# Output projection of the recurrent layer with stationary weights, and its projections emitted in quarters

## The chip, the cores and the metric

The kernel runs on one core of a Trainium2 chip. The metric is the device time of one launch in microseconds; the time before is the median of three runs. A profile is one more execution, taken with the hardware profiler.

## What is computed

Four layers follow one another on x of 2048 rows by 512: A, B, A, B, each on a layer norm of x and added to x.

```python
# layer A: 64 segments of 32 rows, strictly one after the other; M = 8 memory rows, 32 heads of 128
for s in range(n_seg):
    h = concat([mem, x[32*s : 32*s+32]])           # 40 rows
    q, k, v = h @ Wq, h @ Wk, h @ Wv               # 512 -> 32 heads x 128
    p = softmax(mask(q @ k.T * scale))             # 40 x 40 per head
    o = (p @ v) @ Wo                               # 4096 -> 512
    mem = o[:8]; outs.append(o[8:])
# layer B: full attention over 2048 rows, 32 heads of 16
x = x + A(layernorm(x)); x = x + B(layernorm(x))   # and both once more
```

So the memory rows of a segment's result are an input of the next segment's three projections: layer A is a chain of 128 segments in the whole kernel.

## The kernel before

One program holds all four layers. The recurrent chain of layer A is walked segment by segment (`segment`, called by `layer_a`), and the work of layer B is cut into *units* (`emit_qk` L467 and `pv_mm` L487: four score matmuls on four row strips of TensorE, an exponential of 128x2048 in two ScalarE instructions at L481 and L484, and four matmuls that sum up values) which fill the time in which a segment waits. There are 1040 units in all, about half for each B layer. Those of the first run beside the first A layer and, what is left, in a stretch between the A layers; those of the second run beside the second A layer and in a tail after it. Everything that is needed once per 128 rows (layer norm, the rows' projections of layer B, the residual) stands in *chains* (`chain`, `run_chain`), lists of functions that are run one at a time.

TensorE's order is fixed when the program is built. `segment` (L788) holds a list of the segment's steps, `a_pick` takes one of the first six by when its inputs are due on a planner's clock (`Clock`, with one counter per engine), and `step` (L416) decides at every turn whether that step (A), a chain's function (M), a unit's score matmuls (U) or a unit's value matmuls (V) go next. The quota of units per segment comes from the units not yet done. The other engines run in the order in which these functions call them, as far as the scheduler leaves it so. The steps of one segment are, with the index 0 or 1 for the two halves of the 32 heads:

- Q, K, V (`cols` L601): the segment's 32 columns of h are the stationary operand, 512 columns of the weight move, and four such products run in the four 32-column strips of TensorE. Sixteen matmuls make one half of one projection. Its result, 128 rows of 512, is copied out of PSUM by ScalarE or VectorE (`stage`, `evac`).
- X (`turn` L617, `qk_turn` L630): Q and K of a half are turned by eight 128x128 transposes into one PSUM bank and copied by VectorE into `a_KT` and `a_QT`.
- S (`s_group` L646): scores, exponential, row sums, division and 32x32 transposes (L658, L662 to L674).
- P, or A and B where many units are due (`pv_group`, `pv_pair`, `pv_mms` L676): p @ v, four row strips at once, and the copies into `a_OT`.
- O (`o_cols` L707): the product with Wo. The segment's first 32 columns of `a_OT` per head are stationary, 512 columns of Wo move, sixteen matmuls per half, four column strips. Each strip holds the sum over its own eight heads.
- F (`o_fold` L716): the four strips' sums have been copied as fp32 (`a_Op`); four fp32 matmuls with a 0/1 matrix (`c_sel`) add them and turn them, 128 features by 32 rows. VectorE then casts eight of the 32 columns into the next segment's h (L846), and that starts the next segment.

A segment has 40 rows, and a 32-column strip holds 32. The eight rows that don't fit are gathered over four segments: layer norm and projections of these rows in `qk_rest` and the `rest` functions, and for Wo a POOL copy per segment into `a_OX` (L850) and, once per four segments, `o_rest` (two more O rounds, a copy and a fold) at the head of the chain that `tile_done` builds.

```python
PLAN = "Q0 K0 V0 X0 Q1 K1 S0 V1 X1 S1 P0 O0 P1 O1 F0".split()
def o_cols(self, b, rr, lhsT, ready):
    for j in range(4):
        for t in range(4):
            h = 16 * rr + 4 * t + j
            self.nc.tensor.matmul(b.t[32 * t:32 * t + 32, :], lhsT=lhsT(h), rhs=self.Wo[:, h, :], ...)
```

Of the kernel before, what the change touches and what calls it, by code (L numbers as in the profile page):

```python
# [97 lines left out]
class Kern:  # L98
# [21 lines left out]
    def consts(self, mem0):  # L120
# [27 lines left out]
        self.sel32 = cp.tile([128, MAIN], f32, name="c_sel32")  # L148
        nc.vector.tensor_reduce(self.sel32[:], self.identf[:].rearrange("p (t r) -> p r t", t=4), axis=AX.X, op=ALU.add)
# [43 lines left out]
    def a_buffers(self, bp):  # L193
# [16 lines left out]
        self.OX = bp.tile([128, H, 32], bf16, name="a_OX")  # L210
        self.Op = bp.tile([128, 512], f32, name="a_Op")
# [7 lines left out]
    def buffers(self):  # L219
# [4 lines left out]
        self.wbp = self.pool("b_W", bufs=2)  # L224
# [66 lines left out]
    def evac16(self, dst, src, n, ready):  # L291

        self.nc.vector.tensor_copy(dst, src)
        return self.ck.ew("DVE", n // 2, ready)
# [121 lines left out]
    def step(self, ra=INF, ma=None, lead=INF, unit=True):  # L416
# [12 lines left out]
        elif rm <= now and (mode == c.mode() or ma == c.mode() or ra > now or rm < now - 2.5):  # L429
# [139 lines left out]
    def qk_rest(self):  # L569
# [11 lines left out]
        def turn(rr):  # L581
            b, done = self.turn(st[1], st[0])
# [19 lines left out]
    def cols(self, W, lhsT, rr, ready):  # L602

        b, at = self.take()
        for ft in range(4):
# [4 lines left out]
        return b, self.ck.pe(0.87, max(at, ready), "PV", 16) + 0.2  # L610
# [6 lines left out]
    def turn(self, k, q):  # L617
# [3 lines left out]
        for i, (x, _) in enumerate((k, q)):  # L621
            for j in range(4):
                self.nc.tensor.transpose(ps[:, 4 * i + j, :], x[:, 128 * j:128 * j + 128], self.ident[:])  # L623
        return b, self.ck.pe(0.5, max(at, k[1], q[1]), "full", 8)

    def qk_cols(self, h_s, proj, rr):
        b, done = self.cols((self.Wq, self.Wk)[proj], lambda ft: h_s[:, ft, :], rr, self.at.get("mem", 0.0))
        self.staged["QK"[proj], rr] = self.stage(b, done)

    def qk_turn(self, rr):  # L630
        b, done = self.turn(self.staged["K", rr], self.staged["Q", rr])
        ps = b.h(8, 128)
        self.evac16(self.KT[:, rr, :, :, 0:MAIN], ps[:, 0:4].rearrange("p j (t q) -> p j t q", q=MAIN), 512, done)
        b.free = self.at["X", rr] = self.evac16(self.QT[:, rr].rearrange("p j t q -> p j (t q)"), ps[:, 4:8], 512, done)

    def v_round(self, h_s, rr):
        b, done = self.cols(self.Wv, lambda ft: h_s[:, ft, :], rr, self.at.get("mem", 0.0))
        b.free = self.at["V", rr] = self.evac(self.V[:, rr, :], b.t[:], 512, done)
# [68 lines left out]
    def o_cols(self, b, rr, lhsT, ready):  # L707

        for j in range(4):
            for t in range(4):  # L710
                h = 16 * rr + 4 * t + j
                self.nc.tensor.matmul(b.t[32 * t:32 * t + 32, :], lhsT=lhsT(h), rhs=self.Wo[:, h, :],  # L712
                                      start=(rr == 0 and j == 0), stop=(rr == 1 and j == 3), tile_position=(0, 32 * t))
        return self.ck.pe(0.87, ready, "PV", 16) + 0.2

    def o_fold(self, part, ready):  # L716

        b, at = self.take()
        ps = b.f(4, MAIN)
        for ft in range(4):  # L720
            self.nc.tensor.matmul(ps[:, ft, :], lhsT=part[:, 128 * ft:128 * ft + 128], rhs=self.sel32[:], start=True, stop=True)  # L721
        return b, ps, self.ck.pe(0.45, max(at, ready), "full", 4)
# [3 lines left out]
    COST = {"Q": 0.87, "K": 0.87, "V": 0.87, "X": 0.5, "S": 0.5, "P": 0.4, "A": 0.3, "B": 0.3, "O": 0.87, "F": 0.45}  # L726

    def a_ready(self, k, g, left):

        at = self.at  # L730
        if k in "QKV":
            if k != "V" and g and "X0" in left:
                return INF
            t = at.get("mem", 0.0)
        elif k == "X":
            if f"Q{g}" in left or f"K{g}" in left:
                return INF
            t = max(self.staged[p, g][1] for p in "QK")
        elif k == "S":
            if f"X{g}" in left or at["R"] == INF:  # L740
                return INF
            t = max(at["X", g], at["R"])
# [4 lines left out]
        elif k == "O":  # L747
            if f"P{g}" in left or f"A{g}" in left or f"B{g}" in left or (g and "O0" in left):
                return INF
            t = max(at["O", 2 * g], at["O", 2 * g + 1])  # L750
            if g:
                return t
        elif k == "F":
            if "O1" in left:
                return INF
            t = at["part"]
        return max(t, self.bank_at())

    MODE = {"Q": "PV", "K": "PV", "X": "full", "S": "PV", "V": "PV", "P": "S", "A": "S", "B": "S", "O": "PV", "F": "full"}

    def a_pick(self, left):
        now = self.ck.t["PE"] + 0.05
        best = (INF, None)
        for x in left[0:6]:
# [712 lines left out]
```

## Time and profile before

| | before |
|---|---|
| median of three runs | 3594.34 us (3589.13 to 3604.32) |
| the profiled execution | 3603.48 us, span 3601.8 us |
| PE busy | 3118.1 us, 87% of the span |
| ACT busy | 2446.0 us, 68% |
| DVE busy | 1719.0 us, 48% |
| POOL busy | 523.3 us, 15% |
| granted TensorE clock, mean | 0.919 |
| DMA | 371.58 MB, 103 GB/s |

A PE that counts as busy is not at its peak: a matmul's record holds its way through the array, too. The segment's steps can be found by their lines: L608 are Q, K and V, L623 the transposes X, L652 and L658 the scores, L681 the value sums, L712 Wo, L721 the fold. L479, L481, L484 and L493 are the units of layer B, and L465 are matmuls that only keep TensorE at work. A segment reaches from one L846 on DVE to the next.

### The profile page before, as it was taken

What the parts mean: (1) busy time and instruction counts of PE and PEld (TensorE: products, weight loads), DVE (VectorE), ACT (ScalarE), POOL (GpSimd) and SP (SyncE); (2) the same over time, 40 slices, a digit from 0 to 9 for tenths busy, and PEclk for the clock granted to TensorE, in tenths of its full rate; (3) what the DMA queues carried; (4) which work ended last, traced back from release to release, by engine and by line L of the source; (5) the groups of instructions that cost most, each with busy time, mean ns of one, the idle gap of its engine ahead of it and who ended that gap; (6) DMA issues with size and microseconds to landing.
All of it is one profiled execution on the core that took longest, in us unless ns stands there. A gap on an engine that the chain in (4) does not pass through costs nothing.

```text
span 3601.8 us, 136341 instructions
## 1 busy us (share of the span) xinstructions
PE 3118.1 (87%) x59593; PEld 1706.8 (47%) x59611; DVE 1719.0 (48%) x4724; ACT 2446.0 (68%) x3242; POOL 523.3 (15%) x1017
## 2 busy tenths in 40 slices
PE   4888888889898898888898998888988889889898
PEld 2444444444444444444445444444444444446566
DVE  1333333436465655546655553444646565652411
ACT  1333354657676877876698765564867688888898
POOL 1111111112111111111111111111212111110000
PEclk7888888989999998989999998888998999999999
DMA  6111111324243424443524322322425253554331
GB/s 211 37 37 38 49 54 50 101 66 125 88 135 109 148 81 121 139 136 112 154 80 132 96 80 70 91 84 83 137 86 161 85 153 95 167 148 142 106 96 46
DMA packets 375376, 371.58 MB, mean 103 GB/s; under 512 B 72048, under 2 KB 302704, under 8 KB 374768
## 3 DMA queue, kind: packets, MB, share of 16 engines
q1 hardware_dynamic: 334560, 251.31, 24.7%
q0 software_dynamic: 34432, 102.54, 8.4%
q8 instruction: 468, 7.67, 0.9%
q10 hardware_dynamic: 5776, 8.91, 0.8%
q14 instruction: 140, 1.15, 0.1%
HBM read 260.10 MB, written 102.50 MB: 101 GB/s over the span
## 4 chain that ended last, share of the span: by engine, by line
PE 55%; ACT 22%; issue 9%; DVE 8%; DMA 5%; POOL 1%; SPq 0%; ACTq 0%; DVEq 0%; POOLq 0%
PE bank L608 21%; ACT b_pt L481 15%; PE bank L712 9%; PE b_SX L479 7%; PE bank L721 4%; PE b_oacc L493 3%; ACT b_pt L484 3%; DMA b_W<-in_B_wqkv_dram 2%; PE bank L623 2%; PE bank L681 2%; PE bank L1041 1%; ACT a_OT L286 1%; DVE a_PT L672 1%; PE bank L479 1%; DVE a_pn L670 1%
## 5 line engine op out<-in xcount | busy, mean ns | idle before, releaser
L481 ACT ACTIVATE b_pt<-b_SX 128x1536 bf16<-128x1536 f32 (+1 forms) x1040 | 1493.2, 1436 | 429.7 <-PE bank L479 389.1
L484 ACT ACTIVATE b_pt<-bank 128x512 bf16<-128x512 f32 (+1 forms) x1040 | 616.8, 593 | 1.8 <-PE bank L479 1.8
L479 PE MATMUL b_SX<-b_q,b_k 32*128 32x512 bf16 (+3 forms) x4944 | 428.6, 311 | 128.7 <-ACT b_pt L481 110.6
L608 PEld LDWEIGHTS <-a_hT 128*32 128x32 bf16 x12288 | 316.1, 100 | 370.5 <-issue 87.6
L493 PE MATMUL b_oacc<-b_pt,b_v 128*17 128x512 bf16 (+3 forms) x6592 | 422.0, 311 | 12.2 <-ACT b_pt L481 5.8
L479 PE MATMUL bank<-b_q,b_k 32*128 32x512 bf16 (+3 forms) x1648 | 416.1, 312 | 10.2 <-DVE b_xo L1145 5.2
L712 PE MATMUL bank<-a_Wo,a_OT 128*32 128x512 bf16 x4096 | 380.0, 453 | 37.3 <-ACT a_OT L286 34.6
L479 PEld LDWEIGHTS <-b_k 32*128 32x128 bf16 x6592 | 167.7, 92 | 394.4 <-issue 330.4
L608 PE MATMUL bank<-a_Wq,a_hT 128*32 128x512 bf16 x4096 | 299.4, 416 | 15.0 <-DVE a_hT L846 4.8
L288 DVE CAST a_qk<-bank 128x512 bf16<-128x512 f32 x305 | 210.9, 691 | 175.8 <-PE bank L608 158.8
L608 PE MATMUL bank<-a_Wk,a_hT 128*32 128x512 bf16 x4096 | 279.2, 394 | 3.9 <-ACT a_oTa L286 3.9
L608 PE MATMUL bank<-a_Wv,a_hT 128*32 128x512 bf16 x4096 | 265.9, 389 | 12.9 <-ACT a_qk L286 12.6
L288 DVE CAST a_OT<-bank 128x160 bf16<-128x160 f32 x575 | 162.7, 316 | 156.9 <-PE bank L681 155.7
L665 DVE TENSOR_REDUCE a_sm<-a_pn 128x5 f32<-128x200 bf16 x256 | 92.4, 361 | 267.1 <-ACT a_pn L662 266.7
L681 PEld LDWEIGHTS <-a_V 32*128 32x128 bf16 x4096 | 124.8, 93 | 199.8 <-issue 163.2
L943 DVE TENSOR_TENSOR b_ain<-b_oacc,b_ain 128x512 f32<-128x512 f32 (+2 forms) x248 | 164.1, 662 | 103.9 <-PE b_oacc L493 94.0
L712 PEld LDWEIGHTS <-a_OT 128*32 128x32 bf16 x4096 | 126.0, 105 | 183.3 <-issue 54.7
L286 ACT CAST a_qk<-bank 128x512 bf16<-128x512 f32 x207 | 121.1, 587 | 133.6 <-PE bank L608 133.2
L493 PEld LDWEIGHTS <-b_v 128*17 128x17 bf16 x6592 | 126.3, 89 | 169.4 <-issue 127.1
L721 PE MATMUL bank<-c_sel,a_Op 128*128 128x32 f32 x1024 | 163.8, 309 | 44.7 <-ACT a_Op L286 30.7
L721 PEld LDWEIGHTS bank<-c_sel,a_Op 128*128 128x128 f32 x1024 | 149.9, 225 | 97.1 <-ACT a_Op L286 58.5
L948 POOL DMA_DIRECT2D b_A<-b_ain x176 | 95.7, 544 | 675.4 <-DVE b_ain L943 462.2
(139 smaller groups left out, 4484.4 us busy)
## 6 DMA issues: line engine op xcount, KB each, us to landing
b_ain<-b_A SPq DMA_DIRECT2D x224, 256.0 KB
b_W<-in_B_wqkv_dram SPq DMA_DIRECT2D x192, 256.0 KB
b_A<-b_ain POOLq DMA_DIRECT2D x176, 256.0 KB, 2.8
b_q<-b_Q SPq DMA_DIRECT2D x240, 128.0 KB
b_k<-b_K SPq DMA_DIRECT2D x201, 128.0 KB
b_v<-b_V SPq DMA_DIRECT2D x312, 68.0 KB
b_A<-b_aout POOLq DMA_DIRECT2D x80, 128.0 KB, 2.6
a_rest<-a_vx POOLq DMA_DIRECT2D x64, 128.0 KB, 2.2
```

Of the source, the lines that this page charges most:

```text
L286: self.nc.scalar.copy(dst, src)
L288: self.nc.vector.tensor_copy(dst, src)
L479: nc.tensor.matmul(out[t][:, j * qw:(j + 1) * qw], lhsT=k[32 * t:32 * t + 32, kj * 128:(kj + 1) * 128], rhs=q[32 * t:32 * t + 32, 0:qw], s ...
L481: nc.scalar.activation(pt[:, 0:NX, 0:w], self.SX[:, 0:NX, 0:w], ACT.Exp, scale=B_SCALE)
L484: nc.scalar.activation(pt[:, NX + i, 0:w], b.t[:, 0:w], ACT.Exp, scale=B_SCALE)
L493: self.nc.tensor.matmul(self.oacc[32 * t:32 * t + 17, 0:qw], lhsT=u.v[:, kj, 17 * t:17 * t + 17], rhs=u.p[:, t, j * qw:(j + 1) * qw], star ...
L608: self.nc.tensor.matmul(b.t[32 * t:32 * t + 32, :], lhsT=lhsT(ft), rhs=W[:, ft, n * 512:(n + 1) * 512], start=(ft == 0), stop=(ft == 3), t ...
L681: self.nc.tensor.matmul(ps[:, L * h4:L * h4 + L], lhsT=V[32 * t:32 * t + rows, st, h4 * DH:(h4 + 1) * DH], rhs=self.PT[32 * t:32 * t + row ...
L712: self.nc.tensor.matmul(b.t[32 * t:32 * t + 32, :], lhsT=lhsT(h), rhs=self.Wo[:, h, :], start=(rr == 0 and j == 0), stop=(rr == 1 and j == ...
L721: self.nc.tensor.matmul(ps[:, ft, :], lhsT=part[:, 128 * ft:128 * ft + 128], rhs=self.sel32[:], start=True, stop=True)
L943: nc.vector.tensor_tensor(acc[:, w], k.oacc[:, w], acc[:, w], ALU.add)
L948: nc.gpsimd.dma_start(B.Acc_d[self.qc][self.hg][:, self.qo:self.qo + self.qw], acc[:, w])
```

## The change

1. Wo becomes the stationary operand again (`wo_steps`): for every head four 128x128 blocks of Wo are loaded and all 40 columns of `a_OT` move, 128 matmuls per segment that add up in one PSUM bank of 4 x 40 columns. There is no `a_OX`, no `a_Op`, no fold and no `o_rest`; the result stands in PSUM as features by rows, and L846's cast (now L857) reads it directly. The 128 matmuls are four steps W0 to W3 of 32, each for eight heads, ready when those heads' copies into `a_OT` are.
2. Q, K, V and W are emitted in four parts (`col_steps`, `wo_steps`). While a step is open (`active`), a unit's score or value matmuls may go between its parts; a chain's function may only when it has been due for over 2.5 us on the planner's clock.
3. K and Q are turned apart, Y for K and X for Q, each with a PSUM bank of its own; and the copies out of that bank may go to ScalarE where the planner sees it end sooner (`evac16`).
4. The plan is a new one: K before Q, V0 ahead of the first turns, Q1 and V1 behind S0, W0 and W1 behind S1. `a_pick` weighs a step's due time, its place in the list and a change of TensorE's tiling.
5. Buffers: three instead of two for `b_W` (one more load ahead), four instead of two for `a_qk`.

```diff
-        self.OX = bp.tile([128, H, 32], bf16, name="a_OX")
-        self.Op = bp.tile([128, 512], f32, name="a_Op")
...
-        self.wbp = self.pool("b_W", bufs=2)
+        self.wbp = self.pool("b_W", bufs=3)
...
-        self.stp = self.pool("a_stage", bufs=2)
+        self.stp = self.pool("a_stage", bufs=4)
...
     def evac16(self, dst, src, n, ready):
+        ck = self.ck
+        act = max(ck.t["ACT"] - 0.09, ready + 0.04) + ck.cost("ACT", n)
+        dve = max(ck.t["DVE"] - 0.09, ready + 0.04) + ck.cost("DVE", n // 2)
+        if act + self.act_bias < dve - 0.1:
+            self.nc.scalar.copy(dst, src)
+            return ck.ew("ACT", n, ready)
         self.nc.vector.tensor_copy(dst, src)
...
-    def step(self, ra=INF, ma=None, lead=INF, unit=True):
+    def step(self, ra=INF, ma=None, lead=INF, unit=True, busy=False):
...
-        elif rm <= now and (mode == c.mode() or ma == c.mode() or ra > now or rm < now - 2.5):
+        elif rm <= now and (rm < now - 2.5 or not busy and (mode == c.mode() or ma == c.mode() or ra > now)):
             what = "M"
...
+    def col_steps(self, W, lhsT, rr, ready, then):
+        st = {}
+        def part(ft):
+            at = 0.0
+            if ft == 0:
+                st["b"], at = self.take()
+                at = max(at, ready)
+            b = st["b"]
             for t in range(4):
                 n = 4 * rr + t
                 self.nc.tensor.matmul(b.t[32 * t:32 * t + 32, :], lhsT=lhsT(ft), rhs=W[:, ft, n * 512:(n + 1) * 512],
                                       start=(ft == 0), stop=(ft == 3), tile_position=(0, 32 * t))
-        return b, self.ck.pe(0.87, max(at, ready), "PV", 16) + 0.2
+            done = self.ck.pe(0.218, at, "PV", 4) + 0.2
+            if ft == 3:
+                then(b, done)
+        return [lambda ft=ft: part(ft) for ft in range(4)]
...
+    def wo_steps(self, ps, g, ready):
+        def part(i):
+            for h in (8 * g + 2 * i, 8 * g + 2 * i + 1):
+                for ft in range(4):
+                    self.nc.tensor.matmul(ps[:, ft, :], lhsT=self.Wo[:, h, 128 * ft:128 * ft + 128], rhs=self.OT[:, h, :],
+                                          start=(h == 0 and ft == 0), stop=(h == H - 1), skip_group_check=True)
+            self.wo_end = self.ck.pe(0.218, 0.0 if i else ready, "full", 8)
+        return [lambda i=i: part(i) for i in range(4)]
...
-    PLAN = "Q0 K0 V0 X0 Q1 K1 S0 V1 X1 S1 P0 O0 P1 O1 F0".split()
-    PLAN_PAIRS = "Q0 K0 V0 X0 Q1 K1 S0 V1 X1 S1 A0 B0 O0 A1 B1 O1 F0".split()
+    PLAN = "K0 Q0 V0 Y0 X0 K1 S0 Q1 V1 Y1 X1 S1 P0 W0 W1 P1 W2 W3".split()
+    PLAN_PAIRS = "K0 Q0 V0 Y0 X0 K1 S0 Q1 V1 Y1 X1 S1 A0 B0 W0 W1 A1 B1 W2 W3".split()
...
         for x in left[0:6]:
...
-            if t <= now:
-                return t, x
-            best = min(best, (t, x), key=lambda b: b[0])
-        return best if best[1] else (INF, left[0])
+            key = max(t, now) + 0.15 * i + (0.1 if self.MODE[x[0]] != self.ck.mode else 0.0)
+            if key < bk:
+                best, bk = (t, x), key
+        return best
...
-        b.free = self.at["oTa"] = self.evac(self.oTa[:, :, (s % 4) * SEG:(s % 4) * SEG + FRESH], ps[:, :, M:MAIN], 96, end)
-        j = s % 4
-        nc.gpsimd.tensor_copy(self.OX[:, :, 8 * j:8 * j + 8], self.OT[:, :, MAIN:L])
+        wo.free = self.at["oTa"] = self.evac(self.oTa[:, :, (s % 4) * SEG:(s % 4 + 1) * SEG], ps[:, :, M:L], 128, end)
...
-        return k.chain(k.o_rest() + [xo, tr, kk, qq, vv], k.at["OX"], modes="ccffffff")
+        return k.chain([xo, tr, kk, qq, vv], k.at["oTa"])
```

TensorE's order at three places, one row for the first matmul of each step; what repeats is left out.

First place: the second segment of the first A layer, which has no units beside it, from its first projection to its first value sums. Before:

```order
L608 MATMUL bank_246<-a_Wq,a_hT 32x512
...
L608 MATMUL bank_244<-a_Wk,a_hT 32x512
...
L608 MATMUL bank_247<-a_Wv,a_hT 32x512
...
L623 MATMUL bank_246<-c_ident,a_qk 128x128
...
L608 MATMUL bank_244<-a_Wq,a_hT 32x512
...
L608 MATMUL bank_247<-a_Wk,a_hT 32x512
...
L658 MATMUL bank_245<-a_KT,a_QT 32x40
...
L681 MATMUL b_SX<-a_PT,a_V 128x40
```

Now:

```order
L616 MATMUL bank_245<-a_Wk,a_hT 32x512
...
L616 MATMUL bank_242<-a_Wq,a_hT 32x512
...
L616 MATMUL bank_244<-a_Wv,a_hT 32x512
...
L640 MATMUL bank_243<-c_ident,a_qk 128x128
...
L616 MATMUL bank_242<-a_Wk,a_hT 32x512
...
L680 MATMUL bank_244<-a_KT,a_QT 32x40
...
L616 MATMUL bank_243<-a_Wq,a_hT 32x512
...
L616 MATMUL bank_245<-a_Wv,a_hT 32x512
...
L640 MATMUL bank_242<-c_ident,a_qk 128x128
...
L703 MATMUL b_SX<-a_PT,a_V 128x40
```

Before, the row of Wv stands for 32 matmuls, both halves of V; now it stands for 16, and the second half has moved, with that of Q, behind the first scores.

Second place: the end of the same segment, from the scores of the second half on. Before:

```order
L658 MATMUL bank_247<-a_KT,a_QP 32x40
...
L712 MATMUL bank_245<-a_Wo,a_OT 32x512
...
L681 MATMUL bank_246<-a_PT,a_V 128x40
...
L712 MATMUL bank_245<-a_Wo,a_OT 32x512
...
L721 MATMUL bank_244<-c_sel_102,a_Op 128x32 x4
```

Now:

```order
L680 MATMUL bank_245<-a_KT,a_QT 32x40
...
L680 MATMUL bank_245<-a_KT,a_QP 32x40
...
L733 MATMUL bank_242<-a_OT,a_Wo 128x40
...
L703 MATMUL bank_244<-a_PT,a_V 128x40
...
L733 MATMUL bank_242<-a_OT,a_Wo 128x40
```

Each of the two L712 rows stands for 16 matmuls, each of the two L733 rows for 64; behind the last one there is no fold. The segment has 561 of PE's rows before and 752 now.

Third place: the start of a segment of the second A layer with many units beside it. Before:

```order
L608 MATMUL bank_244<-a_Wq,a_hT 32x512
...
L712 MATMUL bank_247<-a_Wo,a_OX 32x512
...
L479 MATMUL b_SX<-b_q,b_k 128x512
...
L493 MATMUL b_oacc<-b_pt,b_v 17x512
...
L608 MATMUL bank_244<-a_Wk,a_hT 32x512
```

Now:

```order
L616 MATMUL bank_245<-a_Wk,a_hT 32x512
...
L481 MATMUL b_SX<-b_q,b_k 128x512
...
L616 MATMUL bank_245<-a_Wk,a_hT 32x512
...
L616 MATMUL bank_243<-a_Wq,a_hT 32x512
...
L481 MATMUL b_SX<-b_q,b_k 128x512
```

Before, a projection's sixteen matmuls stand together, and those of the gathered rows (`a_OX`) are among them; now a unit's scores stand after the first four matmuls of K and again after twelve of Q.

## Rows read from the trace of the kernel before

**Rows 1.** Windows by stretch: length, busy per engine, TensorE's granted clock, DMA share, GB/s.

```profile
82.10:1164.90 1082.80, 929.62 (x17824) 500.67 (x17824) 470.69 (x1371) 567.21 (x916) 160.07 (x315) 0.89 0.25 74
1164.90:1529.10 364.20, 322.32 (x6244) 165.73 (x6236) 206.12 (x525) 291.71 (x355) 60.39 (x117) 0.93 0.41 121
1691.20:2033.30 342.10, 305.28 (x6826) 170.65 (x6828) 204.19 (x552) 280.15 (x325) 52.28 (x101) 0.97 0.44 126
2033.30:2708.20 674.90, 591.92 (x11301) 314.23 (x11306) 325.70 (x909) 426.40 (x628) 104.95 (x205) 0.91 0.29 88
2708.20:3231.10 522.90, 466.58 (x9048) 239.73 (x9041) 315.99 (x800) 433.76 (x510) 92.98 (x179) 0.95 0.46 136
3231.10:3601.80 370.70, 335.35 (x5917) 229.96 (x5923) 95.90 (x275) 321.61 (x351) 21.47 (x38) 0.98 0.33 96
```

**Rows 2.** The same windows for line L846 alone; the count is that of segments.

```profile
82.10:1164.90 1082.80, 9.20 (x48) 0.89 0.25 74
1164.90:1529.10 364.20, 2.71 (x15) 0.93 0.41 121
1691.20:2033.30 342.10, 2.26 (x12) 0.97 0.44 126
2033.30:2708.20 674.90, 5.59 (x30) 0.91 0.29 88
2708.20:3231.10 522.90, 3.80 (x20) 0.95 0.46 136
```

**Rows 3.** Timeline of a segment without units: start, length, instruction, idle before and releaser.

```profile
93.54 0.22 PE L681 MATMUL b_SX<-a_PT,a_V 32*128 32x40 bf16 x3 [1.79 <-DVE a_PT L674]
...
94.57 2.25 PE L712 MATMUL bank<-a_Wo,a_OT 128*32 128x512 bf16 x16
94.61 0.34 ACT L662 ACTIVATE a_pn<-bank 128x200 bf16<-128x200 f32 x1
...
96.37 0.20 DVE L674 STREAM_TRANSPOSE a_PT<-a_pn 128x64 bf16<-128x64 bf16 x1
...
97.28 0.42 ACT L286 CAST a_OT<-b_SX 128x320 bf16<-128x320 f32 x1 [2.34 <-PE bank L681]
...
97.76 1.40 PE L712 MATMUL bank<-a_Wo,a_OT 128*32 128x512 bf16 x16 [0.63 <-ACT a_OT L286]
...
99.20 0.58 ACT L286 COPY a_Op<-bank 128x512 f32<-128x512 f32 x1 [1.49 <-PE bank L712]
...
99.84 1.61 PE L721 MATMUL bank<-c_sel,a_Op 128*128 128x32 f32 x8 [0.68 <-ACT a_Op L286]
101.49 0.19 DVE L846 CAST a_hT<-bank 128x32 bf16<-128x32 f32 x1 [3.42 <-PE bank L721]
```

**Rows 4.** Timeline rows of the same steps at full clock, in two later segments.

```profile
2691.37 1.04 PE L608 MATMUL bank<-a_Wk,a_hT 128*32 128x512 bf16 x16
2699.90 1.13 PE L712 MATMUL bank<-a_Wo,a_OT 128*32 128x512 bf16 x16
...
2739.46 1.08 PE L721 MATMUL bank<-c_sel,a_Op 128*128 128x32 f32 x8
```

**Rows 5.** Timeline rows of short matmuls in strips, and of loads of 128x128 weights.

```profile
2728.62 0.28 PE L658 MATMUL bank<-a_KT,a_QT 128*32 128x40 bf16 x16
2728.72 0.31 PE L658 MATMUL bank<-a_KT,a_QP 128*32 128x40 bf16 x16
...
2689.32 0.45 PEld L623 LDWEIGHTS <-a_qk 128*128 128x128 bf16 x8 [0.42 <-DVE a_qk L288]
```

**Rows 6.** Window of the densest 512 PE instructions found; and the instruction queue: packets, MB, share.

```profile
1934.09:1940.95 6.86, 6.20 (x266) 4.43 (x262) 4.97 (x14) 6.40 (x9) 1.06 (x3) 1.00 0.42 108
...
q8 instruction: 468, 7.67, 0.9%
```

**Rows 7.** Waits: who waited for whom, us in total, times, longest.

```profile
ACT b_pt L481 <- PE bank L479: 389.1, 388, 14.6
```

More of the change, by code (lines that the diff above doesn't have):

```diff
@@ L615, in stage, with turn, qk_steps, then @@
         return t, b.free
-    def turn(self, k, q):
+    def turn(self, xs):
         b, at = self.take()
         ps = b.h(8, 128)
-        for i, (x, _) in enumerate((k, q)):
+        for i, (x, _) in enumerate(xs):
             for j in range(4):
                 self.nc.tensor.transpose(ps[:, 4 * i + j, :], x[:, 128 * j:128 * j + 128], self.ident[:])
[L624 to L638, printed above, removed]
+        return b, self.ck.pe(0.25 * len(xs), max([at] + [r for _, r in xs]), "full", 4 * len(xs)) + 0.15
+    def qk_steps(self, h_s, proj, rr):
+        def then(b, done):
+            self.staged["QK"[proj], rr] = self.stage(b, done)
+        return self.col_steps((self.Wq, self.Wk)[proj], lambda ft: h_s[:, ft, :], rr, self.at.get("mem", 0.0), then)
+    def qk_turn(self, proj, rr):
+        b, done = self.turn([self.staged["QK"[proj], rr]])
+        ps = b.h(8, 128)[:, 0:4]
+        if proj:
+            dst, src = self.KT[:, rr, :, :, 0:MAIN], ps.rearrange("p j (t q) -> p j t q", q=MAIN)
+        else:
+            dst, src = self.QT[:, rr].rearrange("p j t q -> p j (t q)"), ps
+        b.free = self.at["X", proj, rr] = self.evac16(dst, src, 512, done)
+    def v_steps(self, h_s, rr):
+        def then(b, done):
+            b.free = self.at["V", rr] = self.evac(self.V[:, rr, :], b.t[:], 512, done)
+        return self.col_steps(self.Wv, lambda ft: h_s[:, ft, :], rr, self.at.get("mem", 0.0), then)
     def v_place(self, A, s):
@@ L705, in pv_pair @@
         self.at["O", 2 * st + half] = max(b.free for b, _ in bs)
[L707 to L722, printed above, removed]
-    PLAN = "Q0 K0 V0 X0 Q1 K1 S0 V1 X1 S1 P0 O0 P1 O1 F0".split()
-    PLAN_PAIRS = "Q0 K0 V0 X0 Q1 K1 S0 V1 X1 S1 A0 B0 O0 A1 B1 O1 F0".split()
-    COST = {"Q": 0.87, "K": 0.87, "V": 0.87, "X": 0.5, "S": 0.5, "P": 0.4, "A": 0.3, "B": 0.3, "O": 0.87, "F": 0.45}
+    def wo_steps(self, ps, g, ready):
[8 more added lines that the diff above has]
+    PLAN_PAIRS = "K0 Q0 V0 Y0 X0 K1 S0 Q1 V1 Y1 X1 S1 A0 B0 W0 W1 A1 B1 W2 W3".split()
+    COST = {"Q": 0.87, "K": 0.87, "V": 0.87, "X": 0.3, "Y": 0.3, "S": 0.5, "P": 0.4, "A": 0.3, "B": 0.3, "W": 0.87}
     def a_ready(self, k, g, left):
@@ L731, in a_ready @@
         if k in "QKV":
-            if k != "V" and g and "X0" in left:
-                return INF
-            t = at.get("mem", 0.0)
-        elif k == "X":
-            if f"Q{g}" in left or f"K{g}" in left:
-                return INF
[L738 to L742, printed above, removed]
+            t = at.get("mem", 0.0)
+        elif k in "XY":
+            p = "QK"[k == "Y"]
+            if f"{p}{g}" in left:
+                return INF
+            t = self.staged[p, g][1]
+        elif k == "S":
+            if f"X{g}" in left or f"Y{g}" in left or at["R"] == INF:
+                return INF
+            t = max(at["X", 0, g], at["X", 1, g], at["R"])
         elif k == "P":
@@ L800, in segment @@
         done = -min(self.debt, 3.0)
-        while left:
+        active, per = deque(), 0.0
+        while left or active:
             if self.at["VR"] == INF and not chunk.fns:
@@ L808, in segment @@
                 self.qk = self.qk_rest()
-            ra, x = self.a_pick(left)
+            if active:
+                ra, m = ck.t["PE"], self.MODE[x[0]]
+            else:
+                ra, x = self.a_pick(left)
+                m = self.MODE[x[0]]
             lead = quota * (work + 0.4) / total - done
-            what = self.step(ra, self.MODE[x[0]], lead, done < quota and bool(self.next or self.cur or self.runs) and not self.sums_due(left))
+            what = self.step(ra, m, lead, done < quota and bool(self.next or self.cur or self.runs) and not self.sums_due(left), bool(active))
             if what == "U":
@@ L1032, in load @@
                     ws.append(k.wb_load(cuts.popleft()))
-        load(2)
+        load(3)
         def proj():
```

104 lines of the change are left out of this document (39 added, 65 removed).

## The prediction

> **What bounds the kernel now.** I read the windows by stretch first, to see which engine could be the limit where. In the stretches from 82.1 to 1164.9 us and from 2033.3 to 2708.2 us ScalarE is busy 567.2 of 1082.8 and 426.4 of 674.9 us, 52% and 63%; in three others it is busy 80 to 83% (291.7 of 364.2, 280.2 of 342.1, 433.8 of 522.9) [rows 1]. I call the segments of the first kind light, those of the second dense. By the count of the casts that begin a segment there are 48 + 30 = 78 light and 15 + 12 + 20 = 47 dense ones, of 22.6 and 22.5 us, and of 24.3, 28.5 and 26.1 us [rows 2]. What is left of the span, 3601.8 - 2986.9 = 614.9 us, is the loading of the weights, the stretch between the two A layers and the tail, the last with 370.7 us [rows 1]. No A segment, or hardly one, runs there, so the change is worth nothing to them.
>
> In a light segment no engine is full and the chain of waits decides. The timeline of one of 19.4 us shows two places. First, PE stands still for 1.79 us before the first value sums, until the softmax' last transpose releases them. Second, its end: ScalarE's copy into a_OT ends at 97.28 + 0.42 = 97.70 us, then come the O round, the copy of a_Op, the fold, and the next segment's cast at 101.49 us, 3.79 us in which every step waits for the one before [rows 3]. The same round takes 2.25 us right after the idle time and 1.13 us in a later segment; the fold takes 1.61 us here and 1.08 us there [rows 3, 4]. That is TensorE at the 1.2 and at the 2.4 GHz level: the granted clock of the light stretches is 0.89 and 0.91, of the dense ones 0.93 to 0.97 [rows 1].
>
> In a dense segment the units decide. ScalarE is idle 72.5 + 61.9 + 89.1 = 223.5 us in the three stretches [rows 1], 4.8 us for each of 47 segments, and over the whole kernel 389.1 us of its idle time end with a unit's score matmuls [rows 7]: PE was in the middle of something else when the exponential could have begun.
>
> **The change, part by part.** *A pair of W, the disputed price.* No row shows a load of 128x128 weights followed by only 40 columns. Below it is bounded by the scores in four column strips: sixteen pairs start 0.10 us ahead of the next sixteen [rows 5], so a strip, with 128 rows of weights and 40 columns moving, takes a new pair every 25 ns. Above, by the transposes, whose eight full loads stand in 0.45 us; less one load's own 0.1 us that is 0.35 / 7 = 50 ns, but there 128 columns move per load [rows 5]. The work moved is that of the first, and I take 25 ns, so 0.8 us for a step of W and 3.2 us for a segment.
>
> *The tail of a segment.* Removed are a round (1.13), a copy (0.58) and a fold (1.08) [rows 3, 4], with 0.1 us between them 2.9 us at full clock, 3.79 as measured. In its place stand W2 and W3, 64 x 25 ns = 1.6 us, and 0.2 us until the last result can be read, 1.8 us. Like with like that is 1.1 us less. If W runs at half clock in a light segment it is 3.4 against 3.79, 0.4 less; if the denser order holds the clock up, 1.8 against 3.79, 2.0 less.
>
> *W0 and W1* replace the first O round behind the second half's scores. They are hidden there: that half's softmax reaches from 94.61 to 96.57 us, 1.96 us [rows 3], and 64 x 25 ns = 1.6 us end inside. If that cover were gone, all 1.6 us would be on the path. At 31 ns a pair they start to hold up the second value sums.
>
> *The new order in the middle.* V1 (a round is 1.04 us [rows 4]) moves from before the turn into the 1.79 us of idle time, and the first scores no longer wait for Q1; K's turn no longer waits for Q's copy. The most that this can give is the 1.79 us, the least is nothing, if the transposes' copies come late. I take 1.3, V1 and a little of the rest. Late next is the second turn, which PE then does last before the sums.
>
> *Instructions.* A light segment has 752 of PE's rows where it had 561. From the first sums to the end of W3 there are 64 + 72 + 128 + 64 + 128 = 456 in about 6 us. The densest 512 or so of the trace, 266 + 262, took 6.86 us, 13 ns each [rows 6]; 456 at that pace are 5.9 us. They come in packets of 16 KB, 468 of them for the kernel [rows 6]. So the end of the segment is as dense as anything seen. I charge 0.4 us a light segment, between nothing and 1.0.
>
> A light segment then gains 1.1 + 1.3 - 0.4 = 2.0 us.
>
> *Dense segments.* PE's work per segment, with a quarter of the gathered rows' part, was 1.25 x (2 x 1.13 + 1.08) = 4.2 us of records and becomes 3.2 to 6.4. ScalarE is the limit, so what counts is how long an exponential waits for PE. A round in one piece keeps the scores out for 1.04 us, two in a row for 2.1; quarters let them in after 0.26. Of 4.8 us idle I take back 1.5, as the other waits (a bank, a DMA, the end of the segment, where the chain is cut, too) remain; the ends are 0 and 3.
>
> *The rest.* The POOL copy per segment, the extra buffers and the copy of 128 instead of 96 columns are off the path: POOL is busy 160.1 of 1082.8 us [rows 1]. That some turns' copies go to ScalarE costs nothing in light segments, where it is idle nearly half the time; in dense ones VectorE has time, 316.0 of 522.9 us [rows 1], and ScalarE is chosen only if it ends sooner.
>
> **Sum.** 78 x 2.0 + 47 x 1.5 = 156 + 70 = 226 us, or 6.3% of the profiled execution's own 3603.5 us: 3377 us. That execution was 9 us above the median of 3594.3, so I give 3368.
>
> The Trainium skill speaks against the change: its page "TensorEngine Tiling (Array Packing)", section "Performance Considerations", wants stationary and moving operands swapped and columns tiled where the moving side has 64 columns or fewer, which is what the kernel does now. For the product alone the rows agree, 2.3 us for two rounds against 3.2; by the rule one would expect a loss of some 0.9 us a segment. What it leaves out is the copy and the fold that this form needs, 1.66 us by their rows.
>
> **The rivals.** (1) *The clock stays up.* With less idle time light segments no longer fall to half clock: 2.0 in the tail, 1.6 in the middle, less 0.4, is 3.2 x 78 = 250 us, and 47 x 2.0 = 94 in dense ones: 3250. For it speaks the 0.89 of the first stretch; against it, that a segment without units still waits for two softmaxes.
>
> (2) *W at half clock, and instructions late.* W's short matmuls leave TensorE at 1.2 GHz, the tail gives 0.4, and the feed eats most of a middle that gives 1.0: 0.7 x 78 = 55, with 47 x 1.0 = 47 in dense segments: 3492. For it speaks the 2.25 us round in just this place [rows 3].
>
> (3) *A pair takes 50 ns, and the change loses.* Then W0 and W1 take 3.2 us, 1.24 more than the softmax hides, and the tail 3.4 instead of 2.9. With 1.3 won in the middle that is 0.4 us lost per light segment, 34 us; a dense one gets 3.2 us more PE work than I charged, 3.2 - 1.5 = 1.7 lost, 80 us: 3708. It decides from about 40 ns on: the light ones' 2.0 us are used up at 41 (128 x 16 ns), the dense ones' 1.5 at 37. For it speak the transposes, the only full loads in the trace; against it, that strips load 128 rows each 25 ns.
>
> (4) *PSUM banks take it back.* K and Q apart need two banks where one was enough, and Wo's is held from W0 to the end, of four in all. If three or four steps a segment wait 0.5 us for a copy, some 1.8 us, nothing is left: 3594.
>
> **How the numbers follow.** I give the forecast 0.60, (1) 0.08, (2) 0.18, (3) 0.10, (4) 0.04. A measurement of this kernel can tell about 0.5%, 18 us, from no change. Faster by more are the forecast, (1) and (2): 0.86; within it (4): 0.04; slower (3): 0.10. The range takes in the forecast with its bounds (1.0 to 2.8 us a light segment, 0.7 to 2.3 a dense one: 111 to 327 us), most of (2) and the near side of (1): 3260 to 3520 us.
>
> **What would show it.** Right: casts L857 some 17.4 us apart in light segments; 64 matmuls of L733 in 1.6 to 1.8 us; under 0.5 us idle before the first value sums; ScalarE's 389.1 us of waits for scores down to about 320; tail and first 82 us unchanged. Wrong: 64 of L733 in 2.6 us or more; PE idle without a releaser inside W; new waits of turns or scores for a bank; dense stretches as long as before.

## The result and the profile after

The changed kernel takes 3282.5 us, median of four runs (3273.2 to 3289.4), against 3591.7 of the kernel before in the same session: a ratio of 0.913, 95% interval 0.910 to 0.916. The forecast was 3368 us with a range of 3260 to 3520; so the direction and the range hold, and the gain of 309 us is 37% larger than the 226 that I had worked out.

The windows of the kernel after over the same segments as [rows 1] (length, busy time of PE, weight loads, VectorE, ScalarE and POOL with counts, granted clock, DMA share, GB/s):

```profile
80.50:972.00 891.50, 818.91 (x21557) 527.39 (x21560) 448.34 (x1306) 568.19 (x909) 142.15 (x267) 0.97 0.30 89
972.00:1323.00 351.00, 318.93 (x7412) 184.63 (x7412) 195.98 (x506) 304.07 (x366) 55.47 (x105) 0.96 0.45 133
1482.00:1824.50 342.50, 302.75 (x7756) 188.40 (x7752) 194.37 (x530) 279.25 (x327) 46.16 (x86) 0.97 0.42 120
1824.50:2407.30 582.80, 534.14 (x13528) 332.50 (x13528) 310.06 (x868) 412.01 (x606) 93.39 (x175) 0.98 0.34 100
2407.30:2929.80 522.50, 466.62 (x10752) 269.75 (x10744) 295.72 (x756) 456.42 (x545) 86.72 (x162) 0.98 0.47 139
2929.80:3282.30 352.50, 317.90 (x5694) 219.08 (x5686) 95.00 (x273) 303.76 (x330) 19.97 (x35) 0.98 0.34 97
```

The two light stretches went from 1082.8 to 891.5 and from 674.9 to 582.8 us: 283 of the 319.5 us by which the span is shorter, and 3.7 us for each of 77 segments (first cast to last; the forecast's 78 and 47 count the casts in a window and are one too many each). The three dense ones went from 364.2, 342.1 and 522.9 to 351.0, 342.5 and 522.5 us: 13 us in all. The tail lost 18, the rest 5. TensorE's clock in the light stretches rose from 0.89 and 0.91 to 0.97 and 0.98.

The third segment of the first layer in the timeline of the kernel after (start, length, engine and line, tiles, and in brackets the idle time before and its releaser) takes 108.26 - 95.15 = 13.1 us, all of it at full clock. The one of [rows 3] is the second segment and took 19.4 us, as did the third of that kernel; the second of the kernel after, which ends where these rows begin, took 14.6 us, at a mean clock of 0.90.

```profile
95.15 0.19 DVE L857 CAST a_hT<-bank 128x32 bf16<-128x32 f32 x1 [1.49 <-PE bank L733]
...
95.40 1.05 PE L616 MATMUL bank<-a_Wk,a_hT 128*32 128x512 bf16 x16 [0.28 <-DVE a_hT L857]
...
98.10 0.62 PE L640 MATMUL bank<-c_ident,a_qk 128*128 128x128 bf16 x8
...
103.32 1.76 PE L733 MATMUL bank<-a_OT,a_Wo 128*128 128x40 bf16 x64
103.44 0.34 ACT L684 ACTIVATE a_pn<-bank 128x200 bf16<-128x200 f32 x1 [0.18 <-PE bank L680]
...
105.20 0.20 DVE L696 STREAM_TRANSPOSE a_PT<-a_pn 128x64 bf16<-128x64 bf16 x1
...
105.46 0.20 PE L703 MATMUL b_SX<-a_PT,a_V 32*128 32x40 bf16 x3 [0.39 <-DVE a_PT L696]
...
106.46 1.76 PE L733 MATMUL bank<-a_OT,a_Wo 128*128 128x40 bf16 x64 [0.62 <-ACT a_OT L282]
...
108.26 0.19 DVE L857 CAST a_hT<-bank 128x32 bf16<-128x32 f32 x1 [1.49 <-PE bank L733]
```

Three things are to be read here. Two W steps together last 1.76 us, and less the 0.18 us that the record of one such matmul lasts that is 1.58 / 63 = 25 ns from one pair to the next: the price that was in dispute. From W2's start to the next segment's cast it takes 1.80 us; in [rows 3] it is 3.73 from the start of the second O round. Taken over all 77 light segments of the two traces, the same stretch lasts 2.2 us on average, and 3.8 us before. And a projection's sixteen matmuls last 1.05 us at the head of the segment, where those in the segment of [rows 3] ran at half clock, as this row of the timeline of the kernel before shows:

```profile
84.05 1.92 PE L608 MATMUL bank<-a_Wk,a_hT 128*32 128x512 bf16 x16
```

Between, W0 and W1 lie under the second softmax (103.44 to 105.40 us) and hold nothing up: the sums of the second half start 0.06 us after the last transpose. PE's waits for that transpose went down in the whole kernel, here first before and then after (waiting instruction, releaser, us in total, times, longest):

```profile
PE b_SX L681 <- DVE a_PT L674: 73.0, 63, 2.0
```

```profile
PE b_SX L703 <- DVE a_PT L696: 13.0, 22, 2.0
```

ScalarE's wait for scores, 389.1 us before [rows 7], is still 312.1 us (the forecast had about 320):

```profile
ACT b_pt L483 <- PE bank L481: 312.1, 346, 12.3
```

### The profile page after: what moved, and what is told of

Same layout as the page of the kernel before. It is cut to its first block, busy times and chain, and to the rows that moved or that the text cites. A ratio compares the mean times of both kernels' runs of the same rounds, so it can differ in the third digit from the quotient of the medians.

```text
span 3282.3 us, 155872 instructions
## 1 busy us (share of the span) xinstructions
PE 2924.1 (89%) x69448; PEld 1816.7 (55%) x69448; DVE 1638.8 (50%) x4526; ACT 2451.5 (75%) x3245; POOL 474.6 (14%) x889
## 4 chain that ended last, share of the span: by engine, by line
PE 50%; ACT 26%; issue 12%; DMA 5%; DVE 5%; POOL 1%; SPq 1%; ACTq 0%; DVEq 0%; POOLq 0%
ACT b_pt L483 19%; PE bank L616 18%; PE bank L733 9%; PE b_SX L481 8%; ACT b_pt L486 4%; PE b_oacc L495 3%; DMA b_W<-in_B_wqkv_dram 2%; PE bank L640 2%; PE bank L703 2%; PE bank L1028 1%; PE bank L481 1%; ACT a_OT L282 1%; PE bank L680 1%; PE bank L1056 1%; PE b_SX L703 1%
## 5 line engine op out<-in xcount | busy, mean ns | idle before, releaser
L483 ACT ACTIVATE b_pt<-b_SX 128x1536 bf16<-128x1536 f32 (+1 forms) x1040 | 1492.4, 1435 | 361.5 <-PE bank L481 312.1
L733 PE MATMUL bank<-a_OT,a_Wo 128*128 128x40 bf16 x16384 | 503.6, 182 | 58.8 <-ACT a_OT L282 28.7
L733 PEld LDWEIGHTS <-a_Wo 128*128 128x128 bf16 x16384 | 470.3, 98 | 131.4 <-issue 120.8
L616 PE MATMUL bank<-a_Wk,a_hT 128*32 128x512 bf16 x4096 | 290.1, 396 | 25.0 <-DVE a_hT L857 7.8
L616 PE MATMUL bank<-a_Wv,a_hT 128*32 128x512 bf16 x4096 | 280.5, 380 | 14.0 <-ACT a_qk L282 13.4
L616 PE MATMUL bank<-a_Wq,a_hT 128*32 128x512 bf16 x4096 | 286.2, 384 | 2.9 <-ACT a_oTa L282 1.0
L284 DVE CAST a_qk<-bank 128x512 bf16<-128x512 f32 x272 | 186.6, 686 | 176.9 <-PE bank L616 176.5
L282 ACT CAST a_qk<-bank 128x512 bf16<-128x512 f32 x240 | 141.3, 590 | 86.6 <-PE bank L616 84.2
L640 PE MATMUL bank<-c_ident,a_qk 128*128 128x128 bf16 x2048 | 168.8, 220 | 9.1 <-ACT b_pt L486 3.6
L703 PE MATMUL bank<-a_PT,a_V 32*128 32x40 bf16 x2824 | 159.2, 178 | 11.2 <-DVE a_OT L284 2.0
L467 PE MATMUL bank<-c_ident 128*128 128x128 bf16 x2375 | 165.4, 222 | 0.0
```

The source lines that it names most:

```text
L282: self.nc.scalar.copy(dst, src)
L467: self.nc.tensor.matmul(b.t[:, 0:128], lhsT=self.ident[:], rhs=self.ident[:], start=True, stop=True)
L483: nc.scalar.activation(pt[:, 0:NX, 0:w], self.SX[:, 0:NX, 0:w], ACT.Exp, scale=B_SCALE)
L703: self.nc.tensor.matmul(ps[:, L * h4:L * h4 + L], lhsT=V[32 * t:32 * t + rows, st, h4 * DH:(h4 + 1) * DH], rhs=self.PT[32 * t:32 * t + row ...
L733: self.nc.tensor.matmul(ps[:, ft, :], lhsT=self.Wo[:, h, 128 * ft:128 * ft + 128], rhs=self.OT[:, h, :], start=(h == 0 and ft == 0), stop= ...
```

## The experiments

All ratios are against the kernel before, in the same session. A difference in us between two changed kernels is taken across sessions, in which the kernel before had medians from 3591.7 to 3604.8 us; it can be off by some 13 us.

### The stationary Wo alone

The kernel before with part 1 of the change and nothing else: `wo_steps` without parts, no `a_OX`, `a_Op`, `o_fold` or `o_rest`.

```diff
-    PLAN = "Q0 K0 V0 X0 Q1 K1 S0 V1 X1 S1 P0 O0 P1 O1 F0".split()
+    PLAN = "Q0 K0 V0 X0 Q1 K1 S0 V1 X1 S1 P0 W0 W1 P1 W2 W3".split()
...
-        return k.chain(k.o_rest() + [xo, tr, kk, qq, vv], k.at["OX"], modes="ccffffff")
+        return k.chain([xo, tr, kk, qq, vv], k.at["oTa"])
```

> The kernel before with the stationary Wo alone (four whole steps W0 to W3, no gathered rows, no fold), its old order, joint turns, no quarters. Theory 1, the short tail and the vanished gathered-row work are most of the 309 us gained: 3380 to 3430 us, light segments shorter by 2 us or more. Rival, the new order is most of it: the tail gives the 1.1 us of the prediction in 78 light segments, 3490 to 3520 us.

3382.4 us, ratio 0.938 (0.933 to 0.943): 6.2% of the 8.7% that the whole change brings, 222 us less than the 3604.8 of the kernel before in that session. Its two light stretches (windows of the line of the casts: length, VectorE's time in that line, clock, DMA share, GB/s) are 129.1 and 42.6 us shorter than before, 2.2 us a segment. Theory 1 holds.

```profile
78.10:1031.80 953.70, 9.18 (x48) 0.93 0.28 83
1852.70:2485.00 632.30, 5.56 (x29) 0.96 0.33 98
```

### The new order with the old form of Wo

The changed kernel with `o_cols` (in quarters), `o_fold` and `o_rest` put back, and with the old number of buffers for `a_qk` and `b_W`.

```diff
-    PLAN = "K0 Q0 V0 Y0 X0 K1 S0 Q1 V1 Y1 X1 S1 P0 W0 W1 P1 W2 W3".split()
+    PLAN = "K0 Q0 V0 Y0 X0 K1 S0 Q1 V1 Y1 X1 S1 P0 O0 P1 O1 F0".split()
...
-        self.stp = self.pool("a_stage", bufs=4)
+        self.stp = self.pool("a_stage", bufs=2)
```

> The changed kernel with the old form of Wo (columns tiled, gathered rows, fp32 copy and fold; two buffers for a_qk and b_W as before for lack of memory), all else new. Theory 1 (the form of Wo is most of the gain): 3470 to 3520 us. Rival (the order of the steps is most): 3370 to 3420 us, with the idle time before the first value sums gone.

3528.0 us, ratio 0.976 (0.970 to 0.982). The two halves of the change add up, 6.2% + 2.4%, to what they give together. The number lies a little above what theory 1 expected, and far from the rival's. It takes back the extra buffers (part 5 of the change) too, which no run changes alone; the kernel with Wo alone has the old buffers, so its 6.2% do not come from them.

### What of it is the gathered rows

```diff
-        nc.gpsimd.tensor_copy(self.OX[:, :, 8 * j:8 * j + 8], self.OT[:, :, MAIN:L])
...
-        return k.chain(k.o_rest() + [xo, tr, kk, qq, vv], k.at["OX"], modes="ccffffff")
+        return k.chain([xo, tr, kk, qq, vv], k.at["oTa"])
```

> The kernel before without Wo's product for the gathered rows (no copies of these rows, no extra rounds, copy and fold once per four segments); eight of each segment's 32 result rows are left out, as zeros. Theory 1c (of the 210 us that the form of Wo gives alone, the shorter tail is most): 30 to 90 us less than before, 3500 to 3565 us. Rival (the gathered rows' work was most of it): 3420 to 3470 us.

3504.2 us, ratio 0.973 (0.970 to 0.976), 97 us less than the 3601.4 of the kernel before. That is at the upper end of theory 1c and short of the rival: of the 222 us that Wo's form gives, nearly half is the work on rows that didn't fit into a strip. The rest fits the shorter tail: from the start of the second half of Wo to the cast it takes 3.8 us on average in the light segments before and 2.1 in the kernel with Wo alone, and 77 times the difference is 128 us. The forecast had the gathered rows only in the sum of PE's work in dense segments.

### Filler matmuls in the kernel before

```diff
-            if ra == INF:
-                self.keep_warm(t)
+            self.keep_warm(t)
```

> The kernel before, but short filler matmuls on TensorE whenever the planner foresees that a segment's step has to wait, not only when nothing is left to do; nothing else. Theory 2 (half of what light segments gained is the clock, 0.89 before and 0.97 now in the first 48 of them): the granted clock rises to 0.95 or more and 78 light segments gain 1.2 us or more, 3500 us or less. Rival (the clock follows from a shorter chain and is worth little): the clock rises and the time stays within 0.7% of 3592 us, or the fillers stand in the way and it is slower.

3507.7 us, ratio 0.972 (0.968 to 0.977). The windows over the two light stretches of this kernel:

```profile
79.20:1110.30 1031.10, 993.58 (x20545) 616.00 (x20546) 470.15 (x1371) 568.02 (x916) 159.84 (x315) 0.99 0.27 78
1968.30:2618.30 650.00, 621.68 (x12584) 367.41 (x12587) 325.35 (x909) 427.67 (x631) 104.79 (x205) 0.99 0.31 91
```

Against [rows 1] they are 51.7 and 24.9 us shorter, 77 us or 1.0 us a segment, with the clock up from 0.89 and 0.91 to 0.99. Matmuls that compute nothing give 2.8%. Theory 2 asked for 3500 us or less and 1.2 us a segment, and both are just missed; its claim that the clock is half of what the light segments gained falls with it, as 77 of 283 us are about a quarter. What stands is that half clock was a price of its own in the light segments, and that most of it is gone in the changed kernel without more fillers (2375 of them, where the kernel before has 2522 and this one 7665).

### Steps emitted whole, and a mixture

The first kernel empties `active` at once; the second does so unless the segment's quota is 13.

```diff
             work += per
             active.popleft()()
+            while active and quota < 13:
+                work += per
+                active.popleft()()
```

> The changed kernel with each step emitted whole, so that no unit's matmuls go between the parts of a projection or of Wo. The prediction's step (quarters give 1.5 us for each of 47 dense segments): 3282 + 70 = 3350 us, ScalarE's waits for scores up by 50 us or more. Theory 3 (the dense stretches hardly got shorter, so quarters are worth little there): 3270 to 3300 us.

> The changed kernel with steps emitted whole except where a segment's quota of units is 13, which is so in the last segments of the second A layer. Theory 3a (whole steps gain in the stretches around the change of layers, 781 instead of 834 us there, and quarters gain in the last 20 segments with the tail, 875 instead of 894 us): 3225 to 3250 us. Rival (units are only moved between stretches, and their sum stays): 3265 to 3290 us.

Whole steps give 3270.3 us, ratio 0.907 (0.902 to 0.911); the mixture 3255.4, 0.904 (0.897 to 0.911). Beside the changed kernel's 0.913 the quarters thus bring nothing, and against the mixture they cost some 27 us; that step of the prediction falls. Why is in the windows of ScalarE's line of exponentials over the last 20 segments and the tail: first before, then after, then with whole steps (length, ScalarE's time in that line with the count of units, clock, DMA share, GB/s).

```profile
2708.20:3231.10 522.90, 308.81 (x212) 0.95 0.46 136
3231.10:3601.80 370.70, 239.21 (x173) 0.98 0.33 96
```

```profile
2407.30:2929.80 522.50, 322.05 (x222) 0.98 0.47 139
2929.80:3282.30 352.50, 226.61 (x164) 0.98 0.34 97
```

```profile
2376.30:2860.80 484.50, 281.59 (x193) 0.96 0.47 139
2860.80:3270.00 409.20, 270.00 (x193) 0.98 0.34 97
```

With quarters 222 units fit beside the 20 segments, without them 193, and the segments are 38 us shorter then; but the 29 units that don't fit there are done in the tail, which is 57 us longer. The three sums are 893.6, 875.0 and 893.7 us. Around the change of layers it is the other way. Here are the same windows from the 50th segment of the first A layer to the 14th of the second, and over the light stretch that follows, first after, then with whole steps:

```profile
972.00:1824.50 852.50, 495.77 (x348) 0.95 0.44 128
1824.50:2407.30 582.80, 213.56 (x147) 0.98 0.34 100
```

```profile
974.40:1774.70 800.30, 458.90 (x322) 0.96 0.45 131
1774.70:2376.30 601.60, 249.26 (x171) 0.98 0.35 104
```

Whole steps do 26 units fewer there in 52 us less, and the light stretch that takes most of them over is only 19 us longer. A dense stretch can't be read without the place to which its units may move: quarters let a segment take more units, at the price of a longer segment, and of the two places that pays only just ahead of the tail. The mixture, which has them there alone, ends between the two theories' ranges.

### The order, and the turns

The first kernel has the old order of projections and the old rule of choice; the second one turn for K and Q in one bank; the third all copies of turned K and Q on VectorE.

```diff
-    PLAN = "K0 Q0 V0 Y0 X0 K1 S0 Q1 V1 Y1 X1 S1 P0 W0 W1 P1 W2 W3".split()
+    PLAN = "Q0 K0 V0 Y0 X0 Q1 K1 S0 V1 Y1 X1 S1 P0 W0 W1 P1 W2 W3".split()
```

```diff
-    PLAN = "K0 Q0 V0 Y0 X0 K1 S0 Q1 V1 Y1 X1 S1 P0 W0 W1 P1 W2 W3".split()
+    PLAN = "K0 Q0 V0 X0 K1 S0 Q1 V1 X1 S1 P0 W0 W1 P1 W2 W3".split()
```

```diff
     def evac16(self, dst, src, n, ready):
-        if act + self.act_bias < dve - 0.1:
-            self.nc.scalar.copy(dst, src)
-            return ck.ew("ACT", n, ready)
         self.nc.vector.tensor_copy(dst, src)
```

> The changed kernel with the order of steps and the choice among them as before (Q0 K0 V0, turns, Q1 K1, S0, V1; first step that is ready), the rest new. Theory 1a (the idle time before the first value sums goes because V1 and Q1 stand behind S0): it comes back, light segments are longer by 0.8 to 1.3 us, 3340 to 3390 us. Rival (turns apart, copies on ScalarE and the clock took it away): 3300 us or less.

> The changed kernel with K and Q turned together in one bank, as before. Theory 1b (turns apart let K's copy start a half turn earlier, little else): 3285 to 3310 us. Rival 4 of the prediction (the second bank costs as much as it brings): 3270 to 3285 us or less.

> The changed kernel with all copies of turned K and Q on VectorE, as before. The single parts tried so far sum to 210 (Wo) + 40 (order) + 22 (turns apart) - 12 (quarters) = 260 of about 310 us. Theory 4 (the choice of engine for these copies is the rest): 3310 to 3335 us. Rival (the parts help one another, the copies are worth nothing): 3270 to 3295 us.

Old order: 3322.6 us, 0.923 (0.917 to 0.930), so the order with its rule of choice is worth some 40 us, less than the 58 to 108 that theory 1a expected. The idle time before the value sums comes back in part, more of it as a wait for ScalarE than for the transpose. These are the kernel after's other wait, beside the 13.0 us above, and the two of this kernel:

```profile
PE b_SX L703 <- ACT b_pt L483: 10.9, 16, 1.5
```

```profile
PE b_SX L703 <- ACT b_pt L483: 34.3, 38, 1.5
PE b_SX L703 <- DVE a_PT L696: 21.2, 32, 2.0
```

Joint turns: 3304.6 us, 0.918 (0.911 to 0.925), 22 us above the changed kernel, as theory 1b had it, though the two intervals overlap. Copies on VectorE alone: 3352.5 us, 0.932 (0.929 to 0.936), 70 us above. The two light stretches of the three kernels, in the same order (windows of the line of the casts), are 20, 8 and 48 us longer together than the 1474.3 us of the kernel after:

```profile
80.80:990.50 909.70, 9.17 (x49) 0.96 0.30 88
1852.40:2437.00 584.60, 5.55 (x30) 0.98 0.34 100
79.20:980.70 901.50, 9.12 (x49) 0.97 0.30 88
1840.20:2421.00 580.80, 5.55 (x30) 0.99 0.34 101
81.00:1009.50 928.50, 9.12 (x49) 0.96 0.29 87
1865.30:2458.70 593.40, 5.55 (x29) 0.98 0.33 98
```

The copies are the surprise: in the kernel after only 97 of 512 such copies are on ScalarE, as its groups of instructions show (busy time, mean ns, idle before):

```profile
L293 ACT COPY a_KT<-bank 128x512 bf16<-128x512 bf16 x58 | 34.6, 596 | 14.8 <-PE bank L640 14.8
L293 ACT COPY a_QT<-bank 128x512 bf16<-128x512 bf16 x39 | 23.4, 599 | 0.9 <-PE bank L640 0.9
```

With all of them on VectorE, PE waits longer for the softmax' last transpose, which is on that engine too, 30.6 instead of 13.0 us; and the turns themselves wait 18.2 us for ScalarE instead of 3.6, as these rows of the waits show, two of that kernel and then one of the kernel after:

```profile
PE b_SX L698 <- DVE a_PT L691: 30.6, 39, 2.0
PE bank L635 <- ACT b_pt L481: 18.2, 20, 1.3
```

```profile
PE bank L640 <- ACT b_pt L486: 3.6, 7, 0.7
```

Those 18 and 15 us are not 70. If the copies' queue were all of it, sending K's copy to ScalarE in every segment with few units should help further; that was tried last, on the fastest kernel (below).

### Wo's matmuls twice

Each matmul of Wo is followed by one with the same weights, loaded again, that moves 8 columns into unread PSUM columns.

```diff
                     self.nc.tensor.matmul(ps[:, ft, :], lhsT=self.Wo[:, h, 128 * ft:128 * ft + 128], rhs=self.OT[:, h, :], ...)
+                    self.nc.tensor.matmul(ps2[:, ft, :], lhsT=self.Wo[:, h, 128 * ft:128 * ft + 128], rhs=self.OT[:, h, 0:8], ...)
```

> The changed kernel in which each of Wo's 16384 matmuls is followed by one more with the same weights loaded again, which moves only 8 columns into PSUM columns that nobody reads. Theory (25 ns is a floor for a load with its matmul, not the 40 columns' time): 64 + 64 take 3.2 us instead of 1.6; the tail is longer by 1.6 us, W0 and W1 outlast the softmax by 1.2 us, light segments by 2.5 us or more, 3480 to 3560 us. Rival (columns set the price): an added pair costs under 10 ns, 3290 to 3340 us.

3893.9 us, ratio 1.083 (1.075 to 1.091). The floor is shown by the loads of this kernel at full clock (L733 with 40 columns, L735 with 8): they alternate every 25 ns, with 8 columns as with 40.

```profile
93.97 0.10 PEld L733 LDWEIGHTS <-a_Wo 128*128 128x128 bf16 x1
93.99 0.10 PEld L735 LDWEIGHTS <-a_Wo 128*128 128x128 bf16 x1
94.02 0.10 PEld L733 LDWEIGHTS <-a_Wo 128*128 128x128 bf16 x1
94.04 0.10 PEld L735 LDWEIGHTS <-a_Wo 128*128 128x128 bf16 x1
```

The page "TensorE: Matmul & The Clock Gate" of the Trainium skill, section "Back-to-back issue gap", gives about 25 ns as the least distance of two matmuls however few columns move; these rows agree, for matmuls on the whole array. On four strips sixteen start within 0.10 us [rows 5], one every 25 ns in each strip.

But 611 us are lost where theory had 200 to 280, and not in light segments alone. The windows of this kernel over the second light stretch and the last 20 segments:

```profile
2195.10:2909.70 714.60, 675.30 (x17212) 443.33 (x17212) 301.58 (x836) 415.68 (x627) 94.26 (x176) 0.85 0.28 83
2909.70:3552.00 642.30, 593.14 (x13428) 357.78 (x13432) 290.19 (x740) 476.44 (x578) 86.99 (x162) 0.80 0.39 114
```

The last 20 segments are 120 us longer than in the kernel after, 6.0 us each for 128 x 25 ns = 3.2 us of added matmuls. The clock is down to 0.80 from 0.98. So a dense segment, too, gets longer with more work on PE and a slower clock; how much each of the two costs this run doesn't tell apart.

### A faster one

The mixture, with filler matmuls in every foreseen wait and the first two copies into `a_OT` apart; then the same with K's copy always on ScalarE where fewer than six units are due.

```diff
-            if ra == INF:
-                self.keep_warm(t)
+            self.keep_warm(t)
...
-        self.at["O", 2 * st] = self.evac(dst[:, 0:2], self.SX[:, 0:2, 0:w], 2 * w, done)
+        self.at["O", 2 * st] = max(self.evac(dst[:, i], self.SX[:, i, 0:w], w, done) for i in range(2))
```

```diff
+        if proj and self.act_bias == 0.0:
+            b.free = self.at["X", proj, rr] = self.evac(dst, src, 512, done, "ACT")
+        else:
+            b.free = self.at["X", proj, rr] = self.evac16(dst, src, 512, done)
```

> An attempt at a faster one: the changed kernel with quarters only at quota 13, filler matmuls whenever a step is awaited, and the first two copies into a_OT apart, so that two engines share them. Theory 2 (what is left of half clock and the wait of 0.62 us before W2 can be had): 3200 to 3240 us. Rival (the clock is nearly whole already and fillers delay as much as they bring): 3245 to 3270 us.

> The faster attempt (3236 us) with one more rule: where fewer than six units are due in a segment, the copy of the turned K always goes to ScalarE, that of Q by the planner's choice. Theory 4a (sending all copies to VectorE cost 70 us because K's and Q's copies stood one behind the other and before the softmax there; side by side is always better in light segments): 3205 to 3230 us. Rival (the choice by who ends first had already found the places): 3230 to 3255 us.

3236.3 us, ratio 0.899 (0.897 to 0.902): faster than both kernels, 46 us or 1.4% below the changed one. How the last 19 us beyond the mixture divide between fillers and copies was not tried apart. K's copy always on ScalarE in those segments: 3258.1 us, 0.905 (0.902 to 0.908), slower by 22. So theory 4a falls: two engines side by side are not always better. That it is the planner's choice for each copy that helps fits this, but is not shown. What the rest of the 70 us, over half, is made of stays open.

## Why the prediction was right, and where its sizes were off

*The pair of W at 25 ns* was right, and the row that decided it was the nearest one in kind, the short matmuls in strips. Rival (3) needed 40 ns and fell with it.

*The tail* was right as worked out for full clock: 1.8 us were forecast, and 1.80 were measured from W2's start to the next cast. What was mis-sized is what it replaces. I took 2.9 us, like with like at full clock; the light segments really paid 3.8 on average, part of it at half clock, and most of that half clock does not come back: 2.2 us are left, so the tail gives 1.6 us a segment where I had 1.1. With the clock held up by fillers alone the old tail takes 3.3 us on average, and 3.3 - 2.2 is the 1.1 of the forecast. The page "TensorE: Matmul & The Clock Gate" of the Trainium skill, section "The HAM clock gate", puts a cold TensorE at half of its full rate; the rows agree for projections (1.92 and 1.05 us). But a step of W is hit less: 2.29 instead of 1.76 us for 64 pairs in the first segment of the kernel after, which ran at 1.2 GHz. Rival (2) had taken twice.

```profile
74.97 2.29 PE L733 MATMUL bank<-a_OT,a_Wo 128*128 128x40 bf16 x64 [0.51 <-ACT a_OT L282]
```

*The light segments' 2.0 us* were 3.7. The step that was too small is "1.1 + 1.3 - 0.4". Missing in it were the gathered rows, 97 us when left out alone, 63 of them in these stretches; the clock, 77 us there when it alone is held up; and the copies of turned K and Q, for which I had put no gain and which are worth 70, 48 of them here. Too large was the charge for instructions: in the segment shown 456 of them stand in 6.0 us, as close as forecast, and W runs at 25 ns a pair without a break, so of the 0.4 us nothing is to be seen. Rival (1), to which I gave 0.08, had named the clock and came out at 3250, nearer to the 3282 measured than my 3368; but it had 94 us in dense segments, which did not come.

*The middle's 1.3 us* hold in kind and are too many. Most of the idle time before the value sums is gone, as the waits for the transpose show. But order and separate turns, undone one by one, lengthen the light stretches by 20 + 8 us, 0.4 us a segment; the rest of their 40 + 22 us lies in the other stretches.

*The dense segments' 1.5 us* were wrong in kind. A unit's matmuls now go between the quarters, and 10 units more fit beside the last 20 segments; but two of the three dense stretches are as long as before, the sign of being wrong that the prediction names, and with whole steps the kernel is no slower. I had treated ScalarE's idle time in a dense stretch as time that can be had back there; its units can move into the tail, and only the sum of both counts. That sum fell by 19 us.

That the total lies within the range is in part luck: the light segments gave 283 us where the sum had 156, the dense ones 13 where it had 70, and the two errors partly cancel. With the 70 us as well the time would have come to some 3225 us, below the range.

*PSUM banks,* rival (4), took nothing back: undoing the separate turns made the kernel slower, not faster.

Of the 309 us, then, undoing shows for Wo's form (with the extra buffers) 246, for the copies' engine 70, for the order 40, for the turns 22, for the quarters -12. That is 366 and more than the whole; the parts overlap, and that they fill the same waiting time is likely, but not shown.

## What to carry to other kernels

In a chain that one step after another bounds, price an old form by all that hangs on it: the strip-tiled product was the cheaper one by itself, 2.3 against 3.2 us, and its copy, fold and left-over rows made it the dearer one. Where work may move between a full stretch and a later one, judge neither by itself but their sum. And where the granted clock is below 1 in the stretch that you shorten, let one run with filler matmuls say what the clock alone is worth before you forecast the rest.

## What the runs showed of the hardware beyond what was expected

In one run PE had more to do and was granted less clock. With Wo's matmuls doubled, the added half moving 8 columns each, PE had more matmuls than in any other kernel here and was busy 92% of the span, and its granted clock was the lowest: 0.85 and 0.80 in two stretches where the kernel after has 0.98. And a load of 128x128 weights with 40 columns costs 25 ns at 2.4 GHz and 33 ns at 1.2 GHz ((2.29 - 0.20) / 63, the record of one matmul lasting 0.20 us there), a third more and not double. A projection with 512 columns takes nearly twice as long there (1.92 and 1.05 us), so a product in W's form loses less at half clock.
